# Attention before two expert layers: the first scores as a small unit with loads of its own, and a new table of priorities

## The chip, the cores and the metric

The kernel runs on one core of a Trainium2 chip. The metric is the device time of one execution in microseconds (us); less is better.

## What is computed

Three stages follow each other. Attention takes two batches of 12 heads, 448 positions and 64 values a head, with a causal mask. Its output, 896 tokens of 768 values, goes through a product layer (`a*b` with 1536 columns, then `w_out`), and that through a layer of eight experts, of which each token uses one.

```python
scores = scale * np.matmul(q, k.transpose(0, 1, 3, 2))
scores = np.where(mask, -1000000000.0, scores)
attn = np.exp(scores - np.max(scores, axis=-1, keepdims=True))
attn = attn / (np.sum(attn, axis=-1, keepdims=True) + 1e-09)
x = np.matmul(attn, v)          # to (896, 768)
x = (x @ w_a) * (x @ w_b) @ w_out
# for each token the expert with the largest cosine to its embedding:
out[mask] = gate_w[mask, None] * (np.maximum(x[mask] @ w1[e], 0.0) @ w2[e])
```

## The kernel before

**Attention** works on twelve pairs of heads, six pairs to a batch. The loads of a pair are k, q and v (`load`, line 263, on SP's queue); k is scaled by `k_scale` (L423) and v by `v_scale` (L426), then v is split into a high and a low half in 16 bits (`v_hi` L433, `v_lo` L436). A pair's scores come in three units, `UNITS = ((3,), (1,), (2, 0))`: blocks of 112 rows, with 448, 224 and 336 + 112 columns for each of the two heads. `scores` (L470, and L474 for the mask) writes a unit to one of two PSUM tiles named `sc`; in the orders below `sc72` is the third unit of pair 7. `maxima` (L485, VectorE) and `exps` (L501, ScalarE) follow, then the block is transposed, either on TensorE (`turn` L510, `p_out` L523, `p_rest` L528, which makes the low half) or by DMA (`p_hi` L533 or L535, `p_lo` L538, `xturn` L542), and multiplied with V (`pv`, L555 to L557) into `po`, of which there is one: the next pair's first product waits until `weigh` (L577, VectorE) has read it.

**The border between the batches.** When the six pairs of a batch are weighed into `x0`, `squares` (L605 on ScalarE, L607 on VectorE), `norm` (L616 to L621) and `x_scale` (L626, L628) follow, and TensorE transposes the six blocks of 128 columns (`turn_x`, L590; tiles `px00` to `px05` in batch 0, `px10`, `px12` and `px14` with two blocks each in batch 1, in the two `sc` tiles). `x_hi` (L593, ScalarE) and `x_lo` (L597, VectorE) make the halves of x in `bufA`.

**The product layer** begins under attention. `conv_ops` (L330 to L361) turn the 64-bit weights into two halves on VectorE and ScalarE; `mm` (L640, "ab" in this text) is its matmul, 36 to a unit (a block of columns, for one half of the tokens). Four units of the first half of the tokens, 144 matmuls, can run before attention has ended. Then attention's PSUM pool `psA` is closed and a pool `ps` opened over the same eight banks; the first matmul of the second half of the tokens writes to that pool, and needs the x of batch 1.

**The order.** Nothing is scheduled at run time. A planner (`Plan`, from line 57) walks through time with estimated costs, and on each engine picks the ready operation with the lowest rank; the ranks are the table `RANKS`, one number for each operation in the order in which they are declared, and `RK` says which engine takes an operation that several could do. On each engine the instructions then stand in that order, and each waits for its inputs. Where the planner sees TensorE stand still for longer than `LEFT`, `keep_on` (L457) puts in filler matmuls whose result nobody reads ("kept"):

```python
n = int((idle - LEFT) / 0.047)
if pxs or n < 1:
    return
```

`pxs` holds tiles of `turn_x`; it stays filled from `px10` on.

## Time and profile before

| | |
|---|---|
| median of three runs | 518.77 us (516.79 to 519.2) |
| profiled execution, time | 515.67 us |
| profiled execution, span | 514.0 us |
| TensorE busy | 495.6 us (96%) |
| VectorE busy | 407.1 us (79%) |
| ScalarE busy | 203.9 us (40%) |
| GpSimd busy | 129.9 us (25%) |
| chain that ended last, TensorE's share | 80% |

Busy time is the time in which an engine worked on an instruction, so a share near 100% over the whole span says that this engine bounds most of it, not that it bounds every stage. The timeline gives start and duration of instructions in microseconds from the span's start, and in square brackets how long the engine stood idle before and what ended the wait. PE is TensorE's matmul, DVE VectorE, ACT ScalarE, POOL GpSimd, SPq the queue of SyncE, which issues the loads. A matmul's duration overlaps the next one's, so distances between starts tell the rate.

### The profile page before, as it was taken

The numbers are of one execution on the slowest core, as the hardware profiler recorded it, in microseconds if no ns is written. First come the engines' busy times: TensorE is split into PE (matmuls) and PEld (weight loads), VectorE is DVE, ScalarE is ACT, GpSimd is POOL, SyncE is SP. The second block draws the span as 40 slices with busy tenths as digits, with TensorE's granted clock in tenths as the row PEclk, the third lists the DMA queues.
The fourth block names the chain that finished last, engine by engine and source line by source line (L and its number), as shares of the span: only waits on it lengthen the run. The fifth ranks groups of instructions, "written<-read, shape, count | busy, mean of one in ns | idle before, by whom it ended". The sixth has DMA issues, their size and how long they took to land.

```text
span 514.0 us, 12637 instructions
## 1 busy us (share of the span) xinstructions
PE 495.6 (96%) x5128; PEld 336.9 (66%) x5128; DVE 407.1 (79%) x652; ACT 203.9 (40%) x476; POOL 129.9 (25%) x142
## 2 busy tenths in 40 slices
PE   6989799999999999999999999999999999999994
PEld 4666677666555555545557666566887888878883
DVE  5999999998799996899821579895659996986940
ACT  4969899786233322433220111112332133132232
POOL 7688975621000000000000000000512243131432
PEclk9999999999999999999999999999999999999998
DMA  8989776636065563889730168883387879767731
GB/s 243 280 194 259 196 127 133 144 127 110 14 219 209 187 195 113 192 192 271 204 62 3 63 227 316 313 297 139 99 318 227 304 221 342 242 217 260 223 107 48
DMA packets 67067, 98.14 MB, mean 191 GB/s; under 512 B 44390, under 2 KB 47462, under 8 KB 66992
## 3 DMA queue, kind: packets, MB, share of 16 engines
q1 hardware_dynamic: 65088, 89.28, 59.6%
q0 software_dynamic: 1904, 7.90, 4.8%
q8 instruction: 43, 0.70, 0.6%
q14 instruction: 32, 0.26, 0.2%
HBM read 79.46 MB, written 7.97 MB: 170 GB/s over the span
## 4 chain that ended last, share of the span: by engine, by line
PE 80%; DVE 6%; ACT 5%; POOL 3%; DMA 3%; issue 2%; another core or an unknown queue 0%; POOLq 0%; SPq 0%; DVEq 0%; ACTq 0%
PE ab L640 27%; PE x L1051 16%; PE py L1310 12%; PE ph L1257 4%; PE ph L1259 4%; PE ph L1258 4%; PE sc L470 3%; ACT pr L501 3%; PE pt L510 1%; DVE cv L354 1%; DVE cv L350 1%; PE px L590 1%; DMA woT<-woc 1%; DMA ld<-in_v_dram 1%; PE po L557 1%
## 5 line engine op out<-in xcount | busy, mean ns | idle before, releaser
L640 PE MATMUL ab<-bufA 128*128 128x448 f16 x864 | 167.7, 352 | 0.0
L640 PEld LDWEIGHTS <-bufA 128*128 128x128 f16 x864 | 83.3, 98 | 74.4
L1051 PE MATMUL x<-woc,gL 128*128 128x512 f16 x336 | 56.5, 326 | 0.0
L1157 POOL DMA_INDIRECT x<-xse,gidi x1 | 1.1, 1093 | 218.3 <-DVE bufB L1031 218.3
L501 ACT ACTIVATE pr<-sc,mn 112x336 f32<-112x336 f32 (+2 forms) x96 | 46.7, 504 | 11.5 <-DVE mn L485 11.5
L1051 PEld LDWEIGHTS <-gL 128*128 128x128 f16 x336 | 32.4, 98 | 21.0
L470 PE MATMUL sc<-ld,ld 64*112 64x448 f32 (+3 forms) x192 | 33.2, 444 | 7.2 <-DMA ld<-in_q_dram 4.1
L354 DVE SCALAR_TENSOR_TENSOR cv<-raw,cv 128x768 uint32<-128x768 uint32 x36 | 36.2, 1005 | 0.4
L350 DVE SCALAR_TENSOR_TENSOR cv<-raw,cv 128x768 uint32<-128x768 uint32 x36 | 35.2, 977 | 0.9
L1310 PEld LDWEIGHTS <-hh 128*128 128x128 f16 (+1 forms) x256 | 26.9, 112 | 12.3
L485 DVE TENSOR_REDUCE mn<-sc 112x2 f32<-112x896 f32 (+3 forms) x48 | 33.8, 727 | 0.8 <-PE sc L474 0.7
L1035 DVE SCALAR_TENSOR_TENSOR bufC<-rw,bufC 128x768 f16<-128x768 f32 (+1 forms) x28 | 32.6, 1165 | 1.4
L1035 DVE SCALAR_TENSOR_TENSOR bufB<-rw,bufB 128x768 f16<-128x768 f32 (+1 forms) x28 | 32.5, 1159 | 1.4
L1035 DVE SCALAR_TENSOR_TENSOR bufA<-rw,bufA 128x768 f16<-128x768 f32 (+1 forms) x28 | 31.9, 1138 | 1.4
L648 DVE TENSOR_TENSOR asb<-asb,ab 128x448 f32<-128x448 f32 x24 | 14.9, 619 | 22.2 <-PE ab L640 21.2
L1267 POOL TENSOR_TENSOR hl<-hr,hh 128x512 f16<-128x512 f32 (+2 forms) x20 | 21.9, 1096 | 35.6 <-ACT hr L1266 29.9
L1057 ACT ACTIVATE row<-x 128x768 f16<-128x768 f32 x7 | 5.7, 810 | 62.2 <-PE x L1051 53.3
L1031 DVE TENSOR_SCALAR bufC<-rw 128x768 f16<-128x768 f32 (+1 forms) x28 | 19.6, 701 | 11.9 <-DMA rw<-in_moe_w_dram 6.1
L1265 ACT ACTIVATE hh<-ph 128x512 f16<-128x512 f32 (+2 forms) x20 | 10.4, 522 | 46.0 <-PE ph L1259 46.0
L1051 PE MATMUL x<-woc,gE 128*128 128x512 f16 (+1 forms) x168 | 28.4, 326 | 0.0
L557 PE MATMUL po<-vh,tbuf 112*128 112x64 f16 x240 | 25.4, 194 | 2.1 <-DVE tbuf L528 2.1
L555 PE MATMUL po<-vh,tbuf 112*128 112x64 f16 x240 | 25.7, 194 | 0.3 <-DVE x L577 0.3
(263 smaller groups left out, 1201.2 us busy)
## 6 DMA issues: line engine op xcount, KB each, us to landing
rw<-in_moe_w_dram SPq DMA_DIRECT2D x36, 512.0 KB, 5.6
rw<-in_moe_w_dram SPq DMA_DIRECT2D x48, 384.0 KB, 4.2
raw<-in_moe_w_a_dram SPq DMA_DIRECT2D x12, 768.0 KB, 4.5
raw<-in_moe_w_b_dram SPq DMA_DIRECT2D x12, 768.0 KB, 4.7
raw<-in_moe_w_out_dram SPq DMA_DIRECT2D x12, 768.0 KB, 5.4
ld<-in_k_dram SPq DMA_DIRECT2D x12, 224.0 KB, 4.2
ld<-in_q_dram SPq DMA_DIRECT2D x12, 224.0 KB, 3.6
ld<-in_v_dram SPq DMA_DIRECT2D x12, 224.0 KB, 3.9
```

What stands on the lines that cost most here:

```text
L350: nc.vector.scalar_tensor_tensor(t, r()[:, :, 1], 0xC0000000, t, op0=ALU.bitwise_and, op1=ALU.bitwise_or)
L354: nc.vector.scalar_tensor_tensor(t, r()[:, :, 0], 29, t, op0=ALU.logical_shift_right, op1=ALU.bitwise_or)
L470: nc.tensor.matmul(sc[:CP, j, o : o + W], qt[hd, c * CP : W], kt[hd, :W], start=n == 0, stop=False)
L485: nc.vector.tensor_reduce(mns[pi][:, c, :], sc[:CP, :, o : o + W], axis=AX.X, op=ALU.min)
L501: nc.scalar.activation(pr[:, d : d + W], sc[:CP, jj, o : o + W], AF.Exp, bias=mn[:, c, jj : jj + 1], scale=-1.0, accum_out=sums[pi][:, c, ...
L555: nc.tensor.matmul(po[:, c, jj, :], ph, vh[:, kc, jj, :], start=kc == 0, stop=False)
L557: nc.tensor.matmul(po[:, c, jj, :], pl_, vh[:, kc, jj, :], start=False, stop=kc == c)
L640: nc.tensor.matmul(gt[i][:, :S], w[:, h, i, kc, :], x[:, kc, ts], start=kc == n == 0, stop=kc == KC - 1 and n == 2)
L1035: nc.vector.scalar_tensor_tensor(dl, R.pop(("raw", j, pc))[:, :n], SE, dh, op0=ALU.mult, op1=ALU.subtract)
L1051: nc.tensor.matmul(xp[:, ns], G(f)[:, a, tk], woc[:, f, l, ns], start=st, stop=sp)
L1267: nc.gpsimd.tensor_tensor(lv, hr, hv, op=ALU.subtract)
L1310: nc.tensor.matmul(py[:n, ns], a[:, f, :n], w_[:, f, ns], start=k < 2 and f == 0 and w_ is w2h, stop=a is htl and f == FC - 1)
```

## The change

Two small loads come first on SP's queue, into a tile `kq0` of their own: the first 224 columns of k and 112 columns of q of the first pair. The second unit of pair 0 takes its operands from them and waits for no other load; a small scale on VectorE (line 685 of the new text, 0.28 in the planner's costs) goes with it. The planner gets a further dependence: the evacuation of a transposed block, and the DMA transpose, wait for the weighing of two pairs before. `LEFT` goes from 0.35 to 0.3. The whole table of ranks is replaced, and some picks of engines in `RK`: seven casts of the high half leave ScalarE (five to GpSimd, two to VectorE), and three squares and one scaling of x go from ScalarE to VectorE. Of the table one row stands here.

```diff
-        -72.3, -61.4, -49.8, -89.5, -68.3, 44.1, -52.2, -222.3, 35.3, -81.4, -88.6, 62.4, -14, -64.5, 38.1, -54.8,
+        -60.8, 13.2, -56.1, -42.9, -19.6, -8.9, -121.7, -13.3, -57.2, -95.7, 61.4, -45.4, 91.9, -128.9, -55.9,
...
+    kq0 = ap.tile([P, 3 * CP], F32, name="kq0", bufs=1)
+    nc.sync.dma_start(kq0[:, : 2 * CP], k[0, 0][:, : 2 * CP])
+    nc.sync.dma_start(kq0[:, 2 * CP :], q[0, 0][:, CP : 2 * CP])
     for i in (1, 0, 2):
         load(0, i)
...
-    LEFT = 0.35
+    LEFT = 0.3
...
-                nc.tensor.matmul(sc[:CP, j, o : o + W], qt[hd, c * CP : W], kt[hd, :W], start=n == 0, stop=False)
+                if (pi, u) == (0, 1):
+                    lhs, rhs = kq0[hd, 2 * CP :], kq0[hd, : 2 * CP]
+                else:
+                    lhs, rhs = qt[hd, c * CP : W], kt[hd, :W]
+                nc.tensor.matmul(sc[:CP, j, o : o + W], lhs, rhs, start=n == 0, stop=False)
...
+    kq_o = op("SP", 0.7, lambda: None, rank=-101)
+    kq_o = op("DVE", 0.28, lambda: nc.vector.tensor_scalar(kq0[:, : 2 * CP], kq0[:, : 2 * CP], SQ, None, op0=ALU.mult), kq_o, rank=-101)
...
-            sc_o[pi, u] = so = op("PE", SCOST[u], lambda pi=pi, u=u: scores(pi, u), k_o[pi], ld_[pi, 0],
+            sc_o[pi, u] = so = op("PE", SCOST[u], lambda pi=pi, u=u: scores(pi, u), *((kq_o,) if (pi, u) == (0, 1) else (k_o[pi], ld_[pi, 0])),
                                   rank=r0 + rk, ring=rsc)
...
-                    done = op("SP", 1.25, lambda g=g: xturn(g), l_o[g], rank=g - 20, ring=rtb)
+                    done = op("SP", 1.25, lambda g=g: xturn(g), l_o[g], wg_o.get(pi - 2), rank=g - 20, ring=rtb)
```

How the instructions move is shown at three places. The line numbers of the new text are 4 to 10 higher than those before.

**VectorE at the start.** `ld1_0`, `ld0_0` and `ld2_0` are k, q and v of pair 0, `ld2_1` is v of pair 1, and `mn0` are the maxima of pair 0. Before:

```order
L423 TENSOR_SCALAR ld1_0_87<-ld1_0_87 128x448
L426 TENSOR_SCALAR ld2_0_91<-ld2_0_91 112x512
L485 TENSOR_REDUCE mn0_174<-sc00_159 112x2
L426 TENSOR_SCALAR ld2_1_154<-ld2_1_154 112x512
L436 TENSOR_TENSOR vl0_177<-ld2_0_91,vh0_176 112x512
L485 TENSOR_REDUCE mn0_174<-sc01_169 112x2
```

Now:

```order
L685 TENSOR_SCALAR kq0_87<-kq0_87 128x224
L427 TENSOR_SCALAR ld1_0_90<-ld1_0_90 128x448
L493 TENSOR_REDUCE mn0_168<-sc01_160 112x2
L430 TENSOR_SCALAR ld2_0_94<-ld2_0_94 112x512
L493 TENSOR_REDUCE mn0_168<-sc00_174 112x2
L430 TENSOR_SCALAR ld2_1_166<-ld2_1_166 112x512
L440 TENSOR_TENSOR vl0_191<-ld2_0_94,vh0_190 112x512
```

The maxima of the small unit stand ahead of the scale of v; those of the large unit (`sc00`) stand behind that scale, as before.

**VectorE and TensorE at the border between the batches.** On VectorE, `pt30` is the first transposed block of pair 6, and L528 (L536 in the new text) makes the low half that the first product of pair 6 needs; `x0_0<-po5` is the weighing of pair 5. Before:

```order
L577 TENSOR_TENSOR x0_0_431<-po5_1077,rr5_1092 112x4x128
L607 SCALAR_TENSOR_TENSOR junk_149,nsq0_150<-x0_0_431 112x128
L528 TENSOR_TENSOR tbuf6_122<-pt30_1142,tbuf6_122 112x448
L485 TENSOR_REDUCE mn7_1226<-sc70_1201 112x2
L616 TENSOR_TENSOR n0sq_75<-nsq0_150 112x4
```

Now:

```order
L536 TENSOR_TENSOR tbuf6_125<-pt30_1151,tbuf6_125 112x448
L585 TENSOR_TENSOR x0_0_490<-po5_1120,rr5_1072 112x4x128
L615 SCALAR_TENSOR_TENSOR junk_152,nsq0_153<-x0_0_490 112x128 x2
L493 TENSOR_REDUCE mn7_1235<-sc70_1207 112x2
L624 TENSOR_TENSOR n0sq_75<-nsq0_153 112x4
```

On TensorE, `px00` is the first transpose of x. Before:

```order
L457 LDWEIGHTS idb_98
L457 MATMUL kept_191<-maskb_102,idb_98 112x112
L590 MATMUL px00_1305<-id32_93,x0_0_431 128x112 x4
L470 MATMUL sc72_1312<-ld1_7_889,ld0_7_859 112x336 x2
L470 MATMUL sc72_1312<-ld1_7_889,ld0_7_859 112x112 x2
L474 LDWEIGHTS idb_98
L474 MATMUL sc72_1312<-maskb_102,idb_98 112x224
L474 LDWEIGHTS idb_98
L474 MATMUL sc72_1312<-maskb_102,idb_98 112x224
```

Now:

```order
L478 MATMUL sc71_1281<-ld1_7_850,ld0_7_872 112x224 x2
L482 LDWEIGHTS idb_101
L482 MATMUL sc71_1281<-maskb_105,idb_101 112x112
L482 LDWEIGHTS idb_101
L482 MATMUL sc71_1281<-maskb_105,idb_101 112x112
L478 MATMUL sc72_1291<-ld1_7_850,ld0_7_872 112x336 x2
L478 MATMUL sc72_1291<-ld1_7_850,ld0_7_872 112x112 x2
L482 LDWEIGHTS idb_101
L482 MATMUL sc72_1291<-maskb_105,idb_101 112x224
L482 LDWEIGHTS idb_101
L482 MATMUL sc72_1291<-maskb_105,idb_101 112x224
L563 LDWEIGHTS tbuf7_127
```

The low half of `pt30` stands ahead of the weighing of pair 5. On TensorE the third unit of pair 7 and one block times V (of which the first rows are shown) stand ahead of `px00`; before, they stood behind it.

**TensorE at the end of batch 1**, with the semaphores for which an instruction waits. Before, ab matmuls of the first half of the tokens (`ab210`) stand on both sides of `px14`:

```order
L640 LDWEIGHTS bufA_74
L640 MATMUL ab210_2232<-bufA_74 128x448
L590 MATMUL px14_2255<-id32_93,x0_1_1427 128x112 [waits DVE_49,PE_49]
L590 MATMUL px14_2255<-id32_93,x0_1_1427 128x112 x7
L640 LDWEIGHTS bufA_74
L640 MATMUL ab210_2232<-bufA_74 128x448
```

Now the last of the first half (`ab310`) stands ahead of `px14`, and the first of the second half (`ab001`) behind it:

```order
L648 LDWEIGHTS bufA_74
L648 MATMUL ab310_2246<-bufA_74 128x448
L598 MATMUL px14_2296<-id32_96,x0_1_1421 128x112 [waits DVE_49,PE_49]
L598 MATMUL px14_2296<-id32_96,x0_1_1421 128x112 x7
L648 LDWEIGHTS bufA_74 [waits DVE_49,PE_49]
L648 MATMUL ab001_2344<-bufA_74 128x448 [waits Activation_49]
```

90 ab matmuls stood ahead of `px10` and 104 ahead of `px14`; now 139 and 144 do. In the new program `ab001` lies in the second of the two PSUM banks of `px14`, and the DVE wait of its weight load is for the last low half of x made from `px14`. The filler matmuls are 139 before and 127 now. In front of the norm of batch 0 stand two VectorE instructions more, in front of that of batch 1 fifteen more.

## Rows read from the trace of the kernel before

**Rows 1.** Windows by stage: busy us of PE, PEld, DVE, ACT, POOL; then clock, DMA, GB/s.
```profile
10.00:66.00 56.00, 49.76 (x709) 37.95 (x706) 53.27 (x88) 47.31 (x157) 46.44 (x41) 0.97 0.94 235
66.00:112.00 46.00, 45.81 (x601) 32.28 (x600) 44.87 (x77) 40.57 (x125) 26.11 (x26) 1.00 0.57 124
140.00:500.00 360.00, 359.12 (x3481) 241.77 (x3479) 281.36 (x426) 97.01 (x160) 44.83 (x41) 1.00 0.65 206
```

**Rows 2.** Timeline of the first 8 us: start, us, engine, line, operation [idle before].
```profile
0.82 0.41 SPq L263 DMA_DIRECT2D ld<-in_k_dram  x1
...
1.28 0.42 SPq L263 DMA_DIRECT2D ld<-in_q_dram  x1
...
3.45 0.39 DVE L423 TENSOR_SCALAR ld<-ld 128x448 f32<-128x448 f32 x1 [1.67 <-DMA ld<-in_k_dram]
...
4.14 1.84 PE L470 MATMUL sc<-ld,ld 64*112 64x448 f32 x4 [4.14 <-DMA ld<-in_q_dram]
...
6.27 0.43 DVE L426 TENSOR_SCALAR ld<-ld 112x512 f32<-112x512 f32 x1 [2.42 <-DMA ld<-in_v_dram]
...
7.85 0.63 ACT L501 ACTIVATE pr<-sc,mn 112x448 f32<-112x448 f32 x1 [5.75 <-DVE mn L485]
```

**Rows 3.** Groups by line, first 125 us: the filler matmuls.
```profile
L457 PE MATMUL kept<-maskb,idb 112*112 112x112 bf16 x139 | 10.6, 233 | 0.0
```

**Rows 4.** Timeline of TensorE at the border between the batches.
```profile
58.81 1.01 PE L470 MATMUL sc<-ld,ld 64*112 64x448 f32 x4 [1.01 <-ACT pr L501]
...
62.70 0.23 PE L557 MATMUL po<-vh,tbuf 112*128 112x64 f16 x1 [1.56 <-DVE tbuf L528]
...
63.23 2.56 PE L457 MATMUL kept<-maskb,idb 112*112 112x112 bf16 x25
...
67.40 0.57 PE L590 MATMUL px<-id,x 112*128 112x112 f32 x4
67.91 1.02 PE L470 MATMUL sc<-ld,ld 64*112 64x336 f32 x8
...
69.44 0.57 PE L510 MATMUL pt<-id,pr 112*112 112x112 f32 x4
```

**Rows 5.** Timeline of VectorE at the same border.
```profile
60.17 0.68 DVE L577 TENSOR_TENSOR x<-po,rr 112x512 f32<-112x512 f32 x1
...
62.03 0.61 DVE L528 TENSOR_TENSOR tbuf<-pt,tbuf 112x448 f16<-112x448 f32 x1
```

**Rows 6.** Windows of 2 us there: PE busy, granted clock, DMA share, GB/s.
```profile
62.00:64.00 2.00, 1.30 (x19) 0.62 0.77 230
64.00:66.00 2.00, 2.00 (x23) 0.52 1.50 227
```

**Rows 7.** Timeline of TensorE at the end of batch 1.
```profile
111.65 6.41 PE L640 MATMUL ab<-bufA 128*128 128x448 f16 x33
117.89 1.70 PE L590 MATMUL px<-id,x 112*128 112x112 f32 x16
119.43 2.81 PE L640 MATMUL ab<-bufA 128*128 128x448 f16 x14
122.08 0.93 PE L590 MATMUL px<-id,x 112*128 112x112 f32 x8
122.85 9.44 PE L640 MATMUL ab<-bufA 128*128 128x448 f16 x49
```

**Rows 8.** Timeline of ScalarE and VectorE there: the halves of x.
```profile
123.05 0.98 ACT L593 ACTIVATE bufA<-px 128x448 f16<-128x448 f32 x2 [1.90 <-PE px L590]
...
124.21 1.15 DVE L597 SCALAR_TENSOR_TENSOR bufA<-px,bufA 128x448 f16<-128x448 f32 x2
```

**Rows 9.** Timeline of VectorE and GpSimd: one form of instruction at two times.
```profile
31.97 3.54 POOL L538 TENSOR_TENSOR hl<-pr,hl 112x448 f16<-112x448 f32 x2
...
32.93 1.67 DVE L350 SCALAR_TENSOR_TENSOR cv<-raw,cv 128x768 uint32<-128x768 uint32 x1
...
57.59 0.95 DVE L350 SCALAR_TENSOR_TENSOR cv<-raw,cv 128x768 uint32<-128x768 uint32 x1
```

More of the change, by code (lines that the diff above doesn't have):

```diff
@@ L137, in fused_kernel @@
     RANKS = (
[48 rows of a table removed]
[49 rows of a table added]
     )
-    RK = dict(S=(-2.9, -1.7, 0.6), M=-1.3, T=0.0, H=-5.0, L=-1.6, V=-0.5, sq=6.4, X=-1.6, VIA='PDDPPPDDPPPDDPPPDDPPPDDPPPDDPPPDDPPPDDPPPDDPPPDDPPPDDPPPDDPP', HI='VAAAVVAGAVVAAAVVGAAVVGAAVVAAAVVAAAVVAAAVVAAAVVAAAVVAAAVVGAAV', LO='GGVGGGGVGGGGVGGGGGGGGGVGGGGVGGGGGGGGGGGGGGGGGGGVGGGGGGGGGGGG', SQE='VAAAAVAAAAAAAVAA', XSE='AVVVAVAA', EV='AAAAAAAAAAAAAAAAAAAAAAAAAAAAAAAAAAVAAAAAAAAAAAAAAAAAAAAVAAAA', KS='VGVGGGGGGGGV', VS='VVGGGGGGGGGV', VH='GVGAVAGGGGVG', VL='VGGVGGGGGGVG')
+    RK = dict(S=(-2.9, -1.7, 0.6), M=-1.3, T=0.0, H=-5.0, L=-1.6, V=-0.5, sq=6.4, X=-1.6, VIA='PDDPPPDDPPPDDPPPDDPPPDDPPPDDPPPDDPPPDDPPPDDPPPDDPPPDDPPPDDPP', HI='VAAAVVGGAVVAVAVVGGAVVGAAVVAAAVVAAAVVVGAVVAGAVVGAAVVAGAVVAAAV', LO='GGVGGGGVGGGGGGGGGGGGGGVGGGGVGGGGGGGGGGGGGGGGGGGVGGGGGGGGVGGG', SQE='VAAAVVAAAAAVAVVA', XSE='VVAVVVAA', EV='AAAAAAAAAAAAAAAAAAAAAAAAAAAAAAAAAAAAAAAAAAAAAAAAAVAAAVAAAAAA', KS='VGGGGGGVGGGV', VS='VVGGVGGGGGGG', VH='GVAAGGGGGGVG', VL='VGGVGGGGGGVG')
     NRAW2 = 4
@@ L700, in fused_kernel @@
                     t_o[g] = op("PE", 0.4, lambda g=g: turn(g), e_o[g], rank=g + RK["T"], ring=rpt)
-                    h = op_any("EV", g, {"A": ("ACT", ACTC(S)), "V": ("DVE", DVEC(S))}, lambda g=g, e=EV[g]: p_out(g, e), t_o[g], rank=g + RK["H"], ring=rtb)
+                    h = op_any("EV", g, {"A": ("ACT", ACTC(S)), "V": ("DVE", DVEC(S))}, lambda g=g, e=EV[g]: p_out(g, e), t_o[g], wg_o.get(pi - 2), rank=g + RK["H"], ring=rtb)
                     done = op("DVE", DVEC(S), lambda g=g: p_rest(g), h, rank=g + RK["L"])
```

95 rows, old and new, of the table RANKS are left out of this document.

## The prediction

> **What bounds the kernel now.** I read the windows by stage first, because a share over the whole span mixes stages. TensorE is the bound from about 66 us on: it is busy for 45.81 of the 46 us from 66 to 112, and for 359.12 of the 360 us from 140 to 500 [rows 1]. A microsecond that TensorE loses after 66 us is lost for good, and one gained before is kept, unless TensorE waits again later. Before 66 us it is not the bound: it is busy 49.76 of 56 us, part of that with filler, and VectorE is busy for 53.27 of the same 56 us [rows 1]. VectorE sets the pace of the first batch; ScalarE (47.31) and GpSimd (46.44) have some air.
>
> Then the start [rows 2]. TensorE's first scores begin at 4.14 us, when the whole q of pair 0 has come. VectorE scales k at 3.45 us and then stands until 6.27 us, 2.42 us of it for v of pair 0; the maxima and everything else on VectorE queue behind that. ScalarE's first exponential comes at 7.85 us.
>
> Third, TensorE's standstills. The 139 filler matmuls are busy for 10.6 us, 0.076 us each [rows 3]; they run where a wait was planned. At the border between the batches TensorE waits 1.01 us for exponentials, then 1.56 us for VectorE's low half of a transposed block, and then runs 25 fillers until about 65.8 us [rows 4]. That low half starts at 62.03 us on VectorE, behind the weighing of pair 5 at 60.17 us [rows 5]. After this standstill the granted clock is 0.62 and 0.52 in two stretches of 2 us, so half speed (1.2 instead of 2.4 GHz) for most of both [rows 6].
>
> Fourth, the end of batch 1 [rows 7]. The x of batch 1 is transposed at 117.89 us (px10 and px12, 1.54 us until the next matmul) and at 122.08 us (px14, 0.77 us). In between and behind stand ab matmuls without a gap.
>
> **The change, part by part.** All sums are against the profiled execution, 515.67 us for a span of 514.0 us. It lies 3.1 us under the median of the runs shown (518.77 us), so I add 3.1 at the end.
>
> *The small unit.* Two loads, of k (224 columns) and of q (112), stand first on SP's queue. One issue takes 0.41 us, so k, q and v of pair 0 and all loads behind them are issued some 0.9 us later. From the issue of k at 0.82 us to its use are 2.63 us [rows 2]; the small q, issued at 1.28 us, is there by 3.9 us at that rate, and the unit starts between 3.4 and 3.9 us instead of 4.14: 0.2 to 0.7 us earlier. But VectorE's order (shown above) is the small scale, the k scale, one maximum, and then again the scale of v, which now comes 0.6 to 0.9 us later. VectorE does one maximum more before that wait (0.61 us by the same form) and pays the small scale (0.2 to 0.39, half a row of the k scale or a whole one). What the small unit gives, the later v takes. Ends: 0.7 faster, 0.9 slower; I take 0.3 faster, as ScalarE gets its first exponential about 2 us earlier and is nearly as full as VectorE.
>
> *New priorities from 10 to 66 us.* Counted in the order, VectorE has the same kinds and numbers of instructions in front of the first maximum of pair 4, to within one or two. A new order can only win back what VectorE stands idle, 56 minus 53.27, that is 2.7 us, and can lose as much. Nothing in the order says which, so I take 0. The fillers go from 139 to 127; at 0.076 us that is 0.9 us, but they run inside waits, and dropping one only leaves the wait bare, so this costs and gains nothing.
>
> *The border.* VectorE now makes the low half before the weighing, so TensorE's 1.56 us wait goes [rows 4, 5]. The next thing it waits for is the first transpose of x (67.40 us), whose chain (weighing, squares, norm, scaling) is on VectorE and hardly changes: two instructions more stand before the norm than before, some 0.5 us. In the new order TensorE does the third score unit of pair 7 and one more block times V ahead of that transpose. By the rows these are the 1.53 us from 67.91 to 69.44 us [rows 4]. So 1.5 less 0.5: 1.0 us won. Ends: 0 (the chain is later by all of it) and 2.5 (the wait of 1.56 and the one of 1.01 both go).
>
> *The end of batch 1.* Before, 90 ab matmuls stand ahead of px10 and 104 ahead of px14, so that 40 of the 144 of the first half are left behind px14 to run while the last halves of x are made. Now 139 and 144 stand ahead: nothing is left. Behind px14 comes the first ab matmul of the second half, which lies in the new PSUM pool, in the second bank of px14's own tile; the order shows its weight load waiting for VectorE. So it can't start before the last low half of x is written. From the rows: ScalarE starts on px14 0.97 us after TensorE does (123.05 against 122.08), takes 0.98 us for two blocks [rows 7, 8], then VectorE's second low half takes some 0.6 (two in 1.15), with 0.1 for the handing over: 2.7 us after the start of px14, which itself takes 0.77. TensorE stands for 1.9 us where it is the bound. Before, the same halves were made behind running matmuls, which is why no row shows the wait. Ends: 1.0 (if ScalarE starts after the first half of px14) and 2.7.
>
> px10 itself now waits for the scaled x with 15 more instructions in front of it on VectorE (conversions of weights and products of ab, counted in the order). If VectorE comes no earlier than before, TensorE gives its 1.0 us back here. Ends 0 and 1.0; I take 0.4. A matmul here takes 0.189 us (33 in 6.24), so the 31 between the end of the third unit and px10 cover 5.9 us of this chain [rows 7].
>
> The rest (the added dependence on the weighing two pairs back, the picks of engines, the limit of 0.3) sets the planner's order and adds no instruction; ScalarE gives up seven casts, five to GpSimd, two to VectorE, and four squares and scales go to VectorE, under TensorE after 66 us. I cost it at 0.
>
> **Sum:** -0.3 + 0 - 1.0 + 1.9 + 0.4 = +1.0, so 516.7 us in this execution's terms and **519.8 us** in those of the median. That is no change that a measurement of this kernel can tell: about 0.5%, or 2.6 us, is the least.
>
> **Rivals.**
> - *The clock falls at the end of batch 1 (slower).* The fall of the clock at the border follows the wait of 1.56 us, with one of 1.01 us shortly before; elsewhere from 10 to 500 us the stages show 0.97 to 1.00 [rows 1]. In the two stretches the missing clock is 0.38 and 0.48 of 2 us, 1.7 us together [rows 6]; there it fell on fillers, at the end of batch 1 it would fall on ab matmuls. It decides if the standstill there is 1.6 us or longer. 516.7 + 1.7 = 518.4, or 521.5. Against it: TensorE works without a gap before. 0.20, of which most is over 0.5%.
> - *GpSimd blocks VectorE.* One form on VectorE takes 0.95 us at 57.59 us and 1.67 at 32.93 us, beside two long GpSimd instructions [rows 9]: 0.72 us more. Two of the five casts that go to GpSimd stand before the border: 2 x 0.72 = 1.4 us later, so 518.1, or 521.2. For it: VectorE sets the pace there. 0.13. The Trainium skill (SBUF — State Buffer, section Who interferes with whom) says that VectorE and GpSimd share one port pair as an exclusive lock, and that whichever issues second is blocked; by that rule the order of issue decides, and the trace agrees that the same form takes two durations.
> - *VectorE's idle goes (faster).* If the earlier exponentials let VectorE run through, the 2.7 us come in, and if VectorE is then early at the end of batch 1 too, its two terms shrink: -0.3 - 2.7 - 1.0 + (0 to 2.3) is -4.0 to -1.7, so 511.7 to 514.0, or 514.8 to 517.1. For it: ScalarE's first wait of 5.75 us is the longest of the start. Against it: v comes later. 0.20, most of it over 0.5%.
> - *The small unit does nothing*, because v holds everything or the small q comes no sooner than the whole q did: the forecast without its 0.3, so 517.0, or 520.1, and inside it. The Trainium skill (DMA: Bandwidth & Descriptors, section Specifications) names 512 bytes as the least transfer at line rate, and the small q has rows of 448; no row here shows a load with such rows.
>
> **The numbers.** The forecast has 0.47. Faster by over 0.5% is the better part of the third rival, 0.15; slower by over 0.5% is most of the first, a part of the second and the edge of the forecast, 0.25; the rest, 0.60, is within. The range goes from the third rival's low end, 514.8, to the two slower ones together with the upper end of the start, some 522.8.
>
> **What would show it.** Scores of the small unit at 3.4 to 3.9 us and VectorE waiting for v until about 7 us; the first transpose of x within 1 us of 67.4 us, with the third unit of pair 7 before it; a gap of 1 to 2.7 us in TensorE between px14 and the first ab matmul behind it, ended by VectorE; clock 1.00 behind it. I am wrong if that gap is missing or the transpose of x comes 2 us or more earlier (faster), or if half clock shows after px14 (slower).

## The result, and the profile after

The changed kernel takes **524.48 us** (median of 4 runs, 523.98 to 524.99) against 518.88 us for the kernel before beside it (4 runs, 516.79 to 519.2): **1.0117 times as long, 95% interval 1.0088 to 1.0145** (formed from all the runs, so not quite the quotient of the two medians), slower by some 5.6 us. The forecast was 519.8 us in a range of 514.8 to 522.8; the result lies outside, on the slow side. The profiled executions are 515.67 us (span 514.0) before and 524.99 us (span 523.2) after; they lie 9.2 us of span apart, because the profiled execution of before is shorter than its median and that of after longer.

Windows by stage of the changed kernel (columns as in [rows 1]):

```profile
10.00:66.00 56.00, 49.78 (x723) 37.59 (x722) 52.20 (x89) 45.34 (x150) 49.30 (x43) 1.00 1.01 242
66.00:112.00 46.00, 44.24 (x581) 31.25 (x578) 44.30 (x77) 37.76 (x116) 27.95 (x30) 0.96 0.59 109
112.00:140.00 28.00, 25.02 (x135) 13.39 (x133) 23.39 (x56) 10.43 (x20) 2.17 (x2) 0.94 0.34 109
140.00:500.00 360.00, 356.93 (x3304) 237.25 (x3303) 277.87 (x425) 95.14 (x157) 42.42 (x37) 1.00 0.65 203
```

The first stage is as busy as before. TensorE then loses 1.76 us in 46 where it had lost 0.19 [rows 1], at a clock of 0.96, and 2.98 us in the 28 us from 112 to 140. From 140 to 500 us it loses 3.07 instead of 0.88.

**The start** (timeline, as in [rows 2]):

```profile
3.90 1.09 PE L478 MATMUL sc<-kq 64*112 64x224 f32 x4 [3.90 <-DMA kq<-in_q_dram]
...
6.06 0.45 ACT L509 ACTIVATE pr<-sc,mn 112x224 f32<-112x224 f32 x1 [3.96 <-DVE mn L493]
...
7.16 0.43 DVE L430 TENSOR_SCALAR ld<-ld 112x512 f32<-112x512 f32 x1 [1.14 <-DMA ld<-in_v_dram]
```

The small unit starts 0.24 us before the old first scores, ScalarE 1.8 us earlier, and VectorE waits for v until 7.16 us instead of 6.27.

**The border between the batches.** Timeline of TensorE (compare [rows 4]); then of VectorE and GpSimd, with two rows of batch 1 (from 125 us on) for comparison; and then VectorE before:

```profile
61.10 1.01 PE L478 MATMUL sc<-ld,ld 64*112 64x448 f32 x4 [1.24 <-ACT pr L509]
...
65.72 1.02 PE L478 MATMUL sc<-ld,ld 64*112 64x336 f32 x8
...
69.11 0.57 PE L598 MATMUL px<-id,x 112*128 112x112 f32 x4 [1.70 <-DVE x L636]
...
72.08 1.84 PE L478 MATMUL sc<-ld,ld 64*112 64x448 f32 x4
```

```profile
64.06 0.54 DVE L624 TENSOR_TENSOR n0sq<-nsq 112x4 f32<-112x4 f32 x1
64.63 0.50 DVE L625 TENSOR_SCALAR n0sq<-n0sq 112x4 f32<-112x4 f32 x1
...
65.38 0.53 DVE L628 TENSOR_SCALAR r<-n0sq 112x4 uint32<-112x4 uint32 x1
...
66.02 2.04 DVE L636 TENSOR_SCALAR x<-x,r 112x768 f32<-112x768 f32 x2
67.99 0.38 DVE L543 CAST hl<-pr 112x448 f16<-112x448 f32 x1
68.29 0.19 DVE L577 RECIPROCAL rr<-sums 112x8 f32<-112x8 f32 x1
68.40 0.56 DVE L636 TENSOR_SCALAR x<-x,r 112x768 f32<-112x768 f32 x1
...
125.74 0.15 DVE L624 TENSOR_TENSOR n0sq<-nsq 112x4 f32<-112x4 f32 x1
...
126.62 1.14 DVE L636 TENSOR_SCALAR x<-x,r 112x768 f32<-112x768 f32 x2
...
63.98 0.60 POOL L437 CAST vh<-ld 112x512 f16<-112x512 f32 x1
...
66.25 1.40 POOL L440 TENSOR_TENSOR vl<-ld,vh 112x512 f16<-112x512 f32 x1
```

```profile
63.57 0.15 DVE L616 TENSOR_TENSOR n0sq<-nsq 112x4 f32<-112x4 f32 x1
...
63.95 0.52 DVE L619 TENSOR_SCALAR n0sq<-n0sq 112x4 uint32<-112x4 uint32 x1
...
64.79 2.26 DVE L628 TENSOR_SCALAR x<-x,r 112x768 f32<-112x768 f32 x3
```

The 1.56 us wait for the low half is gone, as forecast, and pair 7's third unit stands ahead of px00, as forecast. But px00 comes at 69.11 us instead of 67.40, behind a new standstill of 1.70 us for VectorE's last scale. Two scales took 2.04 us beside a GpSimd instruction, where two of batch 1 took 1.14; but before, three took 2.26, also beside one (L423 on GpSimd, 1.58 us from 65.06 us on), so most of that is not new. New are two more slow instructions in the norm (three of 0.50 to 0.54 us, before one of 0.52), and a cast and a reciprocal ahead of the third scale. The norm starts 0.49 us later than before (64.06 against 63.57), takes 1.96 us until the first scale instead of 1.22, and from the first scale to the end of the last are 2.94 us instead of 2.26, 0.41 of it for the cast and the reciprocal.

**The end of batch 1.** TensorE (compare [rows 7]); pte is the first matmul behind 180 ab matmuls in both kernels, and from there on the order of every engine is the same in both:

```profile
128.71 1.70 PE L598 MATMUL px<-id,x 112*128 112x112 f32 x16
130.25 1.11 PE L648 MATMUL ab<-bufA 128*128 128x448 f16 x5
131.99 0.96 PE L598 MATMUL px<-id,x 112*128 112x112 f32 x8 [0.63 <-DVE bufA L605]
135.30 8.65 PE L648 MATMUL ab<-bufA 128*128 128x448 f16 x36 [2.35 <-DVE bufA L605]
143.88 0.53 PE L404 MATMUL pte<-id,x 8*128 8x8 f32 x6
```

ScalarE and VectorE behind px14 (compare [rows 8]):

```profile
132.99 0.98 ACT L601 ACTIVATE bufA<-px 128x448 f16<-128x448 f32 x2 [1.45 <-PE px L598]
...
134.00 1.16 DVE L605 SCALAR_TENSOR_TENSOR bufA<-px,bufA 128x448 f16<-128x448 f32 x2 [0.56 <-ACT bufA L601]
```

TensorE at pte before:

```profile
137.32 0.53 PE L400 MATMUL pte<-id,x 8*128 8x8 f32 x6
```

The clock in the changed kernel (windows of 2 us; after the span of each, busy time of PE, PEld, DVE, ACT, POOL, then the granted clock):

```profile
72.00:74.00 2.00, 2.00 (x7) 0.60 (x7) 1.30 (x3) 1.81 (x8) 2.00 (x2) 0.50 0.61 138
...
136.00:138.00 2.00, 2.00 (x6) 0.73 (x5) 1.72 (x10) 0.00 (x0) 0.00 (x0) 0.50 0.06 2
```

Half clock follows both standstills, and here it falls on real work: the score matmul at 72.08 us takes 1.84 us where its like at 61.10 takes 1.01.

**Where the 9.2 us of span went.** Up to px10: 128.71 us with 139 ab ahead of it; 49 of them more than before, at 0.189 us each, are 9.26, so 119.45 against 117.89: 1.56 us. From px10 to pte: 15.17 us and the 9.26 make 24.43, against 19.43: 5.00 us, of which 2.98 are the two standstills and about 1.7 the half clock (36 ab in 8.65 us; the same 36 take 6.97 in the run "bank" below). Behind pte: 379.32 against 376.68, 2.64 us, of which the waits for woT (a tile that DMA fills with a part of w_out, transposed) in the profile's list of waits (in total, times, longest) make 1.9, after and then before:

```profile
PE pW L825 <- DMA woT<-woc: 2.8, 3, 1.5
```

```profile
PE pW L815 <- DMA woT<-woc: 0.9, 1, 0.9
```

### The profile page after: what moved, and what is told of

Its sections match the earlier page's. It is cut to its first block, busy times and chain, and to the rows that moved or that the text cites. A ratio compares the mean times of both kernels' runs of the same rounds, so it can differ in the third digit from the quotient of the medians.

```text
span 523.2 us, 12622 instructions
## 1 busy us (share of the span) xinstructions
PE 498.5 (95%) x5116; PEld 336.3 (64%) x5116; DVE 407.9 (78%) x661; ACT 199.2 (38%) x462; POOL 136.9 (26%) x148
## 4 chain that ended last, share of the span: by engine, by line
PE 74%; DVE 11%; DMA 8%; ACT 2%; issue 2%; POOL 1%; SPq 0%; another core or an unknown queue 0%; POOLq 0%; DVEq 0%; ACTq 0%
PE ab L648 25%; PE x L1061 16%; PE py L1320 11%; PE ph L1269 4%; PE ph L1267 4%; PE ph L1268 4%; PE sc L478 3%; DVE mn L493 2%; DMA woT<-woc 2%; DMA xr<-xs,gidi 2%; DMA ld<-in_v_dram 1%; DMA raw<-in_moe_w_out_dram 1%; DVE tbuf L536 1%; DVE cv L354 1%; DVE cv L358 1%
## 5 line engine op out<-in xcount | busy, mean ns | idle before, releaser
L648 PE MATMUL ab<-bufA 128*128 128x448 f16 x864 | 169.4, 355 | 2.3 <-DVE bufA L605 2.3
L354 DVE SCALAR_TENSOR_TENSOR cv<-raw,cv 128x768 uint32<-128x768 uint32 x36 | 35.1, 976 | 0.9
L493 DVE TENSOR_REDUCE mn<-sc 112x2 f32<-112x448 f32 (+3 forms) x48 | 33.7, 728 | 1.9 <-PE sc L482 1.9
L358 DVE SCALAR_TENSOR_TENSOR cv<-raw,cv 128x768 uint32<-128x768 uint32 x36 | 34.5, 958 | 0.3
L1277 POOL TENSOR_TENSOR hl<-hr,hh 128x512 f16<-128x512 f32 (+2 forms) x20 | 23.2, 1158 | 34.6 <-ACT hr L1276 28.8
L1045 DVE SCALAR_TENSOR_TENSOR bufA<-rw,bufA 128x768 f16<-128x768 f32 (+1 forms) x28 | 30.7, 1096 | 1.4
L652 ACT ACTIVATE asb<-ab 128x448 f32<-128x448 f32 x24 | 13.0, 542 | 35.8 <-PE ab L648 35.8
L565 PE MATMUL po<-vh,tbuf 112*128 112x64 f16 x240 | 25.3, 194 | 1.3 <-DVE tbuf L536 1.3
```

The lines of the kernel that those rows point to most:

```text
L354: nc.vector.scalar_tensor_tensor(t, r()[:, :, 1], 0xC0000000, t, op0=ALU.bitwise_and, op1=ALU.bitwise_or)
L358: nc.vector.scalar_tensor_tensor(t, r()[:, :, 0], 29, t, op0=ALU.logical_shift_right, op1=ALU.bitwise_or)
L493: nc.vector.tensor_reduce(mns[pi][:, c, :], sc[:CP, :, o : o + W], axis=AX.X, op=ALU.min)
L565: nc.tensor.matmul(po[:, c, jj, :], pl_, vh[:, kc, jj, :], start=False, stop=kc == c)
L648: nc.tensor.matmul(gt[i][:, :S], w[:, h, i, kc, :], x[:, kc, ts], start=kc == n == 0, stop=kc == KC - 1 and n == 2)
L1045: nc.vector.scalar_tensor_tensor(dl, R.pop(("raw", j, pc))[:, :n], SE, dh, op0=ALU.mult, op1=ALU.subtract)
```

## The experiments

Theory E: the loss is made at the end of batch 1, where no ab matmul is left to run while the last halves of x are made. Rivals: B, the border with its half clock; S, the small unit and its loads; W, the waits for woT. In several runs the planner is taken out and the tasks are issued in a written list, which is the kernel's own order with only the named tasks moved:

```diff
-            got = [(b[1], e, b[2]) for e in self.free if (b := self.pick(e))]
-            start, eng, o = min(got, key=lambda x: x[:2])
...
+            n = self.written.pop(0)
+            if n < 0:
+                self.still(-n)
+                continue
+            o = self.ops[n]
...
```

A negative number stands for so many fillers. pte is given for each, since it comes before what varies behind it:

| run | median us (runs) | times before, 95% | pte, us |
|---|---|---|---|
| changed | 524.48 (4) | 1.0117 (1.0088 to 1.0145) | 143.88 |
| after_again | 525.34 (4) | 1.0125 (1.0078 to 1.0172) | 144.74 |
| late_px | 522.88 (6) | 1.0111 (1.0075 to 1.0148) | 141.97 |
| late_bank | 520.75 (10) | 1.0065 (1.0032 to 1.0097) | 141.41 |
| bank | 519.98 (12) | 1.0039 (1.0012 to 1.0066) | 140.09 |
| end_fill | 525.98 (6) | 1.0167 (1.0122 to 1.0212) | 142.79 |
| chain_cover | 525.87 (6) | 1.0150 (1.0111 to 1.0189) | 146.15 |
| chain_conv | 523.52 (7) | 1.0091 (1.0063 to 1.0120) | 142.79 |
| border_fill | 526.12 (4) | 1.0175 (1.0096 to 1.0255) | 144.84 |
| x_scale0 | 523.22 (4) | 1.0102 (1.0055 to 1.0150) | 143.72 |
| no_small | 524.91 (4) | 1.0134 (1.0077 to 1.0191) | 142.90 |
| small_alone | 519.42 (12) | 1.0038 (1.0016 to 1.0060) | 141.31 |
| bank_sq | 522.43 (9) | 1.0065 (1.0039 to 1.0092) | 141.41 |
| bank_sq2 | 521.53 (12) | 1.0036 (1.0007 to 1.0064) | 140.23 |
| all_four | 519.18 (12) | 1.0004 (0.9979 to 1.0029) | 139.94 |

The medians of before beside them go from 517.25 to 519.03 us, so the ratio is what compares.

### The end of batch 1

**late_px** puts the loss into the kernel before. Before's list, in which 18 entries (batch 1's turns, x_hi and x_lo) move as one piece:

```diff
- ab 1 to 90, px10, px12, ab 91 to 104, px14, ab 105 to 144
+ ab 1 to 139, px10, px12, px14, ab 140 to 144
```

> The kernel before, its tasks in its own order, but batch 1's 18 turns and halves of x moved behind the 139th ab matmul instead of the 90th and 104th (in the changed kernel they stand behind the 139th and 144th); nothing else is changed. Theory E: a standstill of 2.5 to 3.5 us in front of the first ab of the second half and then the half clock for about 3.5 us, 518.9 + 3 + 1.8 = 523.7 us (522.5 to 525). Rivals B and W: 518.9 (518.4 to 519.5).

Timeline of TensorE in late_px:

```profile
127.61 1.70 PE L659 MATMUL px<-id,x 112*128 112x112 f32 x16
131.66 1.70 PE L659 MATMUL px<-id,x 112*128 112x112 f32 x8 [2.35 <-DVE bufA L666]
133.16 8.88 PE L709 MATMUL ab<-bufA 128*128 128x448 f16 x41
141.97 0.54 PE L470 MATMUL pte<-id,x 8*128 8x8 f32 x6
```

1.0111: this order alone, without the small unit, the table or the picks, costs as much as the whole change, within the intervals. px10 is 0.5 us late by the same count as above (127.61 less 9.26 is 118.35), px10 to pte 4.2 us longer than before. A standstill and half clock are there, but not quite where I expected them: with no ab between px12 and px14 the wait stands in front of px14, for px11's bank.

**bank** leaves the order alone and moves the banks of the new PSUM pool:

```diff
     pW = held("pW")
+    for i in range(2):
+        big("early", i)
```

> The changed kernel with one thing changed: in the new PSUM pool the four banks of the two large tiles are laid out ahead of the two banks for ab, so that the second half's first ab tile lies in a bank that pt has left long before, and no longer in px15's. The order of all engines is the same. Theory P (the standstill of 2.3 us behind px15 is the wait for px15's bank, not for the data): that ab begins right behind px15, its later steps find their halves of x ready, the clock stays at 1.00, the first transposes into pte come at 139.8 us (139 to 141) instead of 143.8 and 144.8, and the time is 3 to 5 us under the changed kernel's (0.7 to 1.2 hundredths above the kernel before become 0 to 0.6). Rival D (it waits for the halves of x themselves, of which the last comes 2.3 us behind px15): within 0.7 us of the changed kernel.

Timeline of TensorE in bank:

```profile
131.97 0.96 PE L598 MATMUL px<-id,x 112*128 112x112 f32 x8 [0.63 <-DVE bufA L605]
132.77 6.97 PE L648 MATMUL ab<-bufA 128*128 128x448 f16 x36
140.09 0.53 PE L404 MATMUL pte<-id,x 8*128 8x8 f32 x6 [0.35 <-DVE x L396]
```

This settles the end of batch 1. px14 stands where it stood (131.97 against 131.99), with the same wait; the standstill of 2.35 us behind it is gone, the 36 ab take 6.97 us, pte is 3.79 us earlier, and the ratio falls from 1.0117 to 1.0039, with intervals that don't touch. So the wait was for px15's bank, not for the halves of x that ab reads: a tile that lies elsewhere can begin with those that are ready. The Trainium skill (PSUM — Partial Sum Buffer, section PSUM bank collisions raise a hardware error) says that the hardware does not stall a matmul that meets another engine's read in a bank, so that the program must guard by bank. The wait in the row is such a guard, and px15's block asks for it too, since the new tile would write over it before it has been read; a tile in another bank needs no wait.

**late_bank** is late_px with the same two lines.

> late_px (the kernel before with batch 1's turns and halves of x behind the 139th ab) with the same layout of the PSUM pool as in the run bank. Theory P: of the 4.2 us that late_px lost between px10 and the first transposes into pte, 3 to 4 come back, pte at 138 to 139.5 us instead of 142.1, the time within 0.4 hundredths of the kernel before. Rival D: as late_px, 1.008 to 1.014 of the kernel before.

Missed: TensorE stands 2.35 us in front of px14, as in late_px, and pte comes at 141.41 us, 0.56 earlier, as px10 does. There the standstill is px14's own, in the old pool, which the layout does not touch. Its ratio is lower (1.0065), but the intervals of the two overlap, and the trace shows no gain at the place in question. Behind pte neither late_bank (377.76 us for 376.71) nor bank (379.70 for 379.32) is shorter, so no trace shows that the layout gains anything elsewhere.

**end_fill** leaves the standstill and fills it:

```diff
+        if (b, kc) == (1, KC - 1):
+            fill = psA.tile([P, 512], F32, tag="pt", name="fill", bufs=2)
+            for _ in range(48):
+                nc.tensor.matmul(fill[:CP, :CP], idb, maskb[:, 0], start=True, stop=True)
```

> The changed kernel with 48 filler matmuls behind px15's transposes, into a PSUM bank of pt that is free by then: they last about 2.25 us at full clock, as long as TensorE stands there now (2.35 us). Theory E with the clock as a part of its price: the clock stays at 1.00 from 134 to 140 us, the first 36 ab of the second half take 6.8 us instead of 8.65, 522.7 us (522.2 to 523.3). If the half clock there isn't brought on by that standstill, or is made up for later: 524.5 (524.0 to 525.0). If the fillers hold TensorE up beyond the stall: up to 525.5.

Timeline of TensorE in end_fill:

```profile
133.38 2.64 PE L602 MATMUL fill<-maskb,idb 112*112 112x112 bf16 x48
135.89 6.97 PE L652 MATMUL ab<-bufA 128*128 128x448 f16 x36
```

The trace bears the clock's part out: with fillers 36 ab take 6.97 us instead of 8.65 (9.84 in after_again), and from px10 to pte are 13.48 us instead of 15.17 (16.36); without the standstill, in bank, 11.40. The time does not: 1.0167, and runs from 522.44 to 528.78. Its list of waits has one that the changed kernel's has not, so part of the time went elsewhere; whether all of it did is open:

```profile
PE ph L1272 <- issue: 2.2, 1, 2.2
```

**chain_cover** tried the other cure: batch 1's chain first, and ab matmuls left behind it.

```diff
+            if b:
+                sq_o[b, part, c].rank = -500
...
+        if b:
+            for o in (no, *xs_):
+                o.rank = -500
...
+            if b:
+                to.rank = ho.rank = lo.rank = -500
...
-    begun = [x for x in unit_o if unit_o[x][0].end is not None]
+    begun = list(unit_o)
```

> The changed kernel with batch 1's squares, norm, scales, turns and halves of x taken first as soon as they are ready (rank -500), and all four first-half units counted as begun, so that 72 of their 144 ab matmuls stand behind px15. Theory E (the loss is made at the end of batch 1: VectorE holds the chain back behind weight conversions, so that only 5 ab matmuls are left to cover the halves of x): px10 at about 115.5 us instead of 128.7, no standstill of TensorE over 0.7 us between px10 and the second half, clock 1.00 there, 518.0 us (516.5 to 519.5). Rival V (VectorE is simply short of time there, and the conversions put behind the chain will be missed later by TensorE): 522 to 525, with waits of ab for bufA L365. Rival B (the loss is made at the border between the batches, 1.7 us in front of px00 and the half clock behind it) and rival W (waits for woT behind 200 us): each leaves this edit at 522.5 to 524.5.

px10 comes at 115.35 us as expected, and the time does not move: rival V. Timelines of TensorE and of VectorE in chain_cover:

```profile
123.28 22.93 PE L648 MATMUL ab<-bufA 128*128 128x448 f16 x106 [2.75 <-DVE bufA L365]
...
122.28 0.95 DVE L365 SCALAR_TENSOR_TENSOR bufA<-cv,bufA 128x768 f16<-128x768 f32 x1
```

The weights of the next unit were now what came late: their last step ran at 122.28 us, behind the whole chain.

**chain_conv** is chain_cover with the conversions' last steps taken ahead of other work.

```diff
+        if 4 <= n < NC1:
+            oe.rank = od.rank = -400
```

> chain_cover with one thing more: the last two steps (ScalarE's L361 and VectorE's L365) of the conversions of weights 4 to 7 take rank -400, so that a finished weight no longer waits behind the chain. Theory V, which came up with chain_cover (the conversions that the chain pushed aside come too late for TensorE): the wait of 2.7 us for bufA L365 and the half clock behind it go, the first transposes into pte come at about 141.5 us instead of 146.1 (143.8 in the changed kernel), and the time is 2 to 4 us under that of the changed kernel on this chip. If VectorE is short of time as a whole: the wait comes at the next unit (weights 6 and 7) instead, pte at 143.5 to 146, no gain over the changed kernel.

Timeline of TensorE in chain_conv:

```profile
121.79 6.98 PE L650 MATMUL ab<-bufA 128*128 128x448 f16 x36 [0.50 <-DVE bufA L365]
129.44 13.41 PE L650 MATMUL ab<-bufA 128*128 128x448 f16 x70 [0.66 <-DVE bufA L365]
```

The wait for weights falls to 1.16 us, the half clock goes, pte comes at 142.79. The time is 1.8 us under after_again's, just short of the 2 to 4 expected, and the intervals overlap. VectorE's order was at fault in chain_cover; a little of the wait stays.

**after_again** is the changed kernel once more.

> The changed kernel once more, beside the kernels of this call and on their chip, as the measure for them, and as a second trace of it. Theory E (end of batch 1) and rival B (border) both expect the same places again: px00 near 69 us with a wait of about 1.7 us, px10 near 128.7, a standstill of 2.3 us in front of the second half's first ab and the half clock behind it; 524.5 us (523 to 527), 1.010 to 1.017 of the kernel before.

px00 (69.75 us, same wait of 1.70), px10 (128.38), both standstills at the end: all repeat. The clock does not: no half clock behind px00, and a longer one at the end (36 ab in 9.84 us).

### The border between the batches

**border_fill** puts 34 fillers in front of px00 (task 261):

```diff
- ..., 336, 443, 261, 340, ...
+ ..., 336, 443, -34, 261, 340, ...
```

> The changed kernel, its tasks in its own order, with 34 more filler matmuls in front of px00, which last about 1.6 us at full clock, as long as TensorE stands there (1.70 us). The clock then stays at 1.00 from 70 to 74 us. Theory E (VectorE's work up to the norm of batch 1 sets px10, whatever TensorE wins at the border): px10 stays near 128.7 us, with a longer wait in front of it (1.7 + about 1), no gain: within 0.5 us of the changed kernel. Rival B (the border's half clock is a part of the loss): px10 and all behind it 1 to 1.7 us earlier.

Timeline of TensorE in border_fill:

```profile
67.90 1.94 PE L529 MATMUL kept<-maskb,idb 112*112 112x112 bf16 x34
69.90 0.60 PE L667 MATMUL px<-id,x 112*128 112x112 f32 x4
...
128.47 1.70 PE L667 MATMUL px<-id,x 112*128 112x112 f32 x16
```

From px00 to px10 are 58.57 us, 1.03 less than the 59.60 of the changed kernel, and 58.63 in after_again, which had no half clock there by itself. So the half clock costs 1.0 us behind px00. But px00 came 0.8 us later than in the first trace, and nothing of it shows in the time, whose interval is wide. px10 comes at 128.47 us, within 0.5 us of the changed kernel's, as theory E had it, but without the wait in front of it that E gave as the reason.

**x_scale0** moves VectorE's last scale (task 257) ahead of the cast (335):

```diff
- ..., 258, 259, 346, 317, 335, 326, 309, 318, 257, ...
+ ..., 258, 259, 346, 317, 257, 335, 326, 309, 318, ...
```

> The changed kernel, its tasks in its own order, with one task moved: at the border between the batches VectorE does its last scale of x directly behind the two others, ahead of the cast of a pr tile and the reciprocal. px00 comes 0.7 to 0.8 us earlier (68.3 to 69.1 us instead of 69.1 and 69.8) and its wait falls from 1.70 to about 1 us. Theory E (px10 is set by VectorE's work up to the norm of batch 1, so the border's stall is absorbed there): px10 within 0.4 us of 128.5, the time within 0.5 us of the changed kernel. Rival B: 0.7 to 2 us faster than the changed kernel, the half clock behind px00 gone.

Timeline of TensorE in x_scale0:

```profile
68.63 0.57 PE L667 MATMUL px<-id,x 112*128 112x112 f32 x4 [1.33 <-DVE x L705]
```

The wait falls by 0.37, not 0.7; the half clock stays, px10 comes at 128.55 and pte at 143.72. Of itself that edit wins next to nothing.

### The small unit

**small_alone** adds the unit alone to the kernel before: the edits at the loads, the scores and the scale from the diff of the change, and before's written list with the unit's tasks first. **no_small** takes the same out of the changed kernel.

> The kernel before with the small unit alone: two small loads ahead of the others, its scale, its scores, minima and exponentials first, all other tasks in the order of before. Theory E: first exponentials at about 6.1 us instead of 7.85, but the first scores of pair 1 come within 0.3 us of where they were, 518.9 us (518.2 to 519.5). Rival S (the two loads and the unit itself cost what was lost): 521 to 524.5. If the start were worth what it wins for ScalarE: 517.1 to 517.8.

> The changed kernel, its tasks in its own order, without the small unit: no small loads and scale, the scores of that unit from the large tiles. Theory E: the same as the changed kernel within 0.7 us. Rival S (the small unit and its loads cost 2 us or more, which the kernel before with the small unit alone, 1.0038 of before, leaves open): 1.5 to 3 us faster than the changed kernel. If the small unit is worth its 1.8 us at the start: up to 1.5 us slower.

In the changed kernel the unit shows no effect: 1.0134 without it, 1.0125 with it, beside the same runs of before, though with these intervals 0.5% either way would not show. In the kernel before it costs 0.4% (1.0016 to 1.0060), some 2 us: more than theory E had (518.2 to 519.5 for 518.9 is at most 1.0012) and just under rival S (521 and more is 1.0040 and more). A window of small_alone (columns as above):

```profile
70.00:72.00 2.00, 2.00 (x12) 1.23 (x10) 1.60 (x3) 1.39 (x3) 1.03 (x1) 0.50 0.00 0
```

In this trace the half clock at the border goes on until past 72 us, where before it ended by 66 us, on fillers [rows 6]. That this makes the 2 us in the other runs too is not shown.

### What is left of the loss

**bank_sq** moves, in bank, the norm of batch 1 ahead (tasks 533 to 537 behind 721, and square 487 to ScalarE).

```diff
- ..., 486, ..., 601, ..., 721, 602, ..., 487, ..., 722, ..., 723, ..., 603, ..., 533, ..., 742, ..., 535, ..., 537, ..., 534, ..., 536, ...
+ ..., 486, 487, ..., 601, ..., 721, 602, 533, 537, 536, 535, 534, ..., 722, ..., 723, ..., 603, ..., 742, ...
```

> The run bank with, besides, batch 1's norm taken earlier: the last square of 640 columns on ScalarE (as in the kernel before) behind its three others instead of on VectorE behind the conversions, and the norm and the four scales right behind the last weight's third conversion step, ahead of ScalarE's gE and asb and of VectorE's gE and last L365. TensorE's order is the same. What is left of the loss in bank before px10 is the wait of about 1.4 to 1.7 us in front of px10 for VectorE's and ScalarE's scales. Theory V2 (that wait comes from where the square and the norm stand on VectorE): px10 at 127.2 us instead of 128.6, no wait in front of it, pte at 138.6 instead of 140.0, the time 1 to 1.5 us under bank's, 1.000 to 1.003 of the kernel before. Rival (VectorE is short of time as a whole: the last weight's L365, now later, is missed by TensorE): px10 at 128 to 129, a wait of ab for bufA L365 of about 1 us, no gain over bank (1.0039).

**bank_sq2** puts the last weight's L365 (603) directly behind the norm (533).

> bank_sq with the last weight's L365 taken directly behind the norm, ahead of VectorE's scales and of its gE. Theory V2 (only the order on VectorE is at fault): no wait of ab for bufA L365 and none of px10 over 0.4 us, px10 at 127.2 us (128.6 in bank, 130.0 in bank_sq), pte at 138.6 us, 1 to 1.5 us under bank's 1.0039 of the kernel before: 1.000 to 1.003. Rival (VectorE is short as a whole): the standstill only moves, px10 at 128 to 129 us, 1.003 to 1.006.

Timelines of TensorE, first in bank_sq, then in bank_sq2:

```profile
127.93 2.25 PE L717 MATMUL ab<-bufA 128*128 128x448 f16 x11 [1.46 <-DVE bufA L435]
```

```profile
110.48 18.52 PE L717 MATMUL ab<-bufA 128*128 128x448 f16 x97
128.83 1.70 PE L667 MATMUL px<-id,x 112*128 112x112 f32 x16
```

Both theories rested on a misreading of mine, and so did the reason that theory E gives in border_fill and x_scale0. The 1.70 in the row of px10 is the length of its 16 transposes, as in the kernel before [rows 7], and no wait: 97 ab matmuls lie between 110.48 and 128.83, at 0.189 us each, without a gap. In this order of TensorE px10 could not come earlier by any work of VectorE, and bank_sq2 stands at bank's ratio (1.0036 and 1.0039). bank_sq only made a wait, for the weight it had put back.

**all_four** adds to bank_sq2 the border's two edits: task 257 ahead as in x_scale0, and 20 fillers in front of px00.

> bank_sq2 with the two edits at the border between the batches besides: VectorE's last scale directly behind the two others (as in x_scale0), and 20 more filler matmuls in front of px00. If the border's loss was only hidden by px10's wait: px10 0.7 to 2 us earlier than in bank_sq2, or as much wait in front of px10 as the border wins; the clock at 1.00 there if the fillers keep it up (border_fill and a second trace of the changed kernel had no half clock there, five others had). Time within 0.3 hundredths of the kernel before, at best 0.998. If VectorE sets px10 also here: px10 as in bank_sq2, with the border's gain as a wait in front of it.

Timeline of TensorE in all_four:

```profile
69.39 0.57 PE L667 MATMUL px<-id,x 112*128 112x112 f32 x4 [0.28 <-DVE x L705]
```

Clock 1.00 from 66 to 74 us, px10 at 128.54, pte at 139.94, and 1.0004 of the kernel before: all of the loss is gone, and nothing is won. In the trace the border gave 0.3 us up to pte; the intervals of bank_sq2 and all_four overlap, so the border's own share of the gain is not settled.

**Still open** is W. Behind pte the order is the same, yet the rest of the span is 376.7 to 377.8 us in the four kernels with before's table, and 378.1 to 380.2 in the twelve traces with the changed one. The waits for woT sum to 2.8 us in one trace of the changed kernel, 2.4 in the other, 3.3 in bank and 1.1 in all_four. With before's table they are 0.8 to 1.1; so all_four has no more of them, and its rest is still 378.25 us: they are not the whole of it. Why those transfers land later was not tried.

## Why the prediction was wrong

- **End of batch 1: right place, too small.** TensorE was to stand 1.9 us behind px14 (1.0 to 2.7), for the last low half of x in the second bank of px14's tile. It stood 2.35 us there, for VectorE's L605, within the bounds; bank shows the cause. The 0.45 us between come from a term that I read wrongly: I counted one low half (0.6 us) behind ScalarE's two high halves, but VectorE makes both behind them (134.00 us, 1.16 us), as it did before (124.21 us, behind 123.05 + 0.98 [rows 8]). What I left out is the 0.63 us in front of px14: with 5 ab instead of 14 between px12 and px14, px11's low half is not ready.
- **px10's wait for the scaled x: wrong.** I took 0.4 us; there was none. VectorE's scales do come late (126.62 us), and behind 90 ab TensorE would have stood there from 119.45 us on; but 139 ab stand ahead, and they run without a gap until px10.
- **Rival 1, the falling clock: right, and wrongly held apart.** I gave it 0.20 because TensorE works without a gap before, and said that it decides from a standstill of 1.6 us. My own sum had 1.9 us there. The condition was met by the forecast itself, so the 1.7 us belonged in the sum: 519.8 + 1.7 = 521.5, inside the range. It came in both traces of the changed kernel, as 1.7 us in one (8.65 against 6.97) and 2.9 in the other (9.84), and it is the last of the signs that I named for being wrong. This is the step that failed most plainly, but not the only one: 521.5 is still 3 us under the measured time.
- **The border: wrong sign.** I forecast 1.0 us won, with 0.5 us more on VectorE. The wait of 1.56 us went, but px00 came 1.7 us late. The norm starts 0.49 us later, which is the number that I had for two more instructions, but by luck: the weighing comes 0.59 us later (60.76 against 60.17 us), behind the low half that now stands ahead of it, and from there to the norm it is 0.10 us less than before. Two things were missing: the cast and the reciprocal in front of the third scale (0.41 us from 67.99 to 68.40), and more of GpSimd beside VectorE. The norm is 0.74 us longer than before. The scales are slow too (two take 1.14 us at 126.62 us and 2.04 at 66.02), but before they were slow as well, and only some 0.3 us of it are new. Together about 1.0 us: that is rival 2, which I had priced (1.4 us) from [rows 9] and thought of for casts ahead of the border, not for the norm and the scales; GpSimd is now busy for 49.30 of the 56 us, where it was for 46.44 [rows 1]. The Trainium skill's rule (SBUF — State Buffer, section Who interferes with whom), one of the two blocks the other on their shared ports, fits the slow rows; the norm's 0.15 us at 63.57 us before, beside a GpSimd scale of 1.48 us from 62.97 us on, shows that not every meeting costs. No run took GpSimd's work away there, so its share is argued and not shown. By the count of ab the kernel is 1.56 us late at px10, where I had it 1.3 early with the start.
- **The small unit: right in the changed kernel** (started at 3.90 us, v's scale 0.9 us later; without it no difference that the runs can tell). That it costs 0.4% in the kernel before was not foreseen.
- **The rest at 0: wrong by some 2 us.** From 140 to 500 us TensorE waits 1.9 us more for woT in the profiled pair, in an order that is the same. I had no term for it, and can't explain it.
- **The top of the range: added up wrongly.** The two slower rivals and the upper end of the start are 519.8 + 1.7 + 1.4 + 1.2 = 524.1, not 522.8. The measured 524.48 lies above that too.

In sum, up to pte: forecast 1.0 us, measured 6.56. Of the 5.56 between them 2.86 arise before px10 (1.56 lost, where start and border were to win 1.3), 0.68 in the standstills (2.98 for 1.9 + 0.4), 1.7 in the clock, and 0.3 can't be placed.

These sums compare one trace with one, and the profiled execution of before is 3.2 us under its median. all_four is as fast as before by its runs (1.0004), and yet its trace has pte 2.62 us later and 4.2 us more span. So up to some 4 of the 9.2 us may lie in which executions were profiled, and what stands here before px10 and behind pte is not loss one for one. The runs' times say it more surely. For the end of batch 1 the forecast had 2.3 us (1.9 + 0.4), and bank takes back 4.0 there (1.0117 less 1.0039): standstills and slow clock. All else was forecast at -1.3 us, and in bank, where it is left, the runs are 2.0 us slower than before (1.0039). Of those 2.0 us no single edit's share is settled.

## What to carry to other kernels

A stall that a change makes where TensorE is the bound should be priced with the slow clock behind it, as one term, if that kernel's own rows show half clock after standstills of such a length. When a new PSUM pool is opened over banks in use, look at which bank its first tile gets: two lines that lay out other tiles first won back two thirds of what this order lost, without changing a single position in it. And keep work that can run at any time for the place behind the last transposes, where it hides the making of their halves: an order that fills every gap early has nothing left to cover the last one. late_px gives the price here, 1.0111 for leaving 5 matmuls there instead of 40.

## What the runs showed of the hardware

- The same order gets half clock in one execution and not in another: behind a standstill of 1.70 us in front of px00 the granted clock was 0.50 from 72 to 74 us in one trace of the changed kernel and 1.00 in the other. In the nine traces with 1.70 or 1.71 us bare in front of px00 it fell in eight. At the end of batch 1 it fell in all seven traces with a bare standstill of 2.35 us. With fillers in the standstill it stayed at 1.00 in each of the three runs that tried them (end_fill there, border_fill and all_four in front of px00).
- VectorE's instructions on four columns took 0.54 us at 64.06 us beside a GpSimd cast and 0.15 at 125.74 us with none beside it, more than three times as long. In the 16 traces the norms have 84 instructions on four columns with no GpSimd operation beside them, none over 0.17 us; of the 76 with one beside them 40 took 0.50 to 0.54 us and 36 no more than 0.17. So the price of such a meeting is not a fixed share of an instruction's length, and not every meeting has one; two scales lost 0.90 us of 2.04.
